# Two heads per quadrant and token pairs for q and k of the last two batches of an attention and highway kernel

## The chip, the cores and the metric

The kernel runs on one core of a Trainium2 chip. The metric is the device time of one execution in microseconds. Before the change it was 151.05 us, the median of 3 runs (151.03 to 151.7).

## The reference

Sliding-window attention with a linear distance bias, and then a highway layer on its output. Batch 8, 8 heads, 576 tokens, head dimension 64, all inputs and the output in float32.

```python
def _attn_ref(q, k, v):                       # each (8, 8, 576, 64)
    window = 128
    scale = 1.0 / np.sqrt(D)
    scores = scale * np.matmul(q, k.transpose(0, 1, 3, 2))
    rel = pos[:, None] - pos[None, :]
    slopes = 2.0 ** (-8.0 * (np.arange(H) + 1) / H)
    bias = slopes[:, None, None] * (-np.abs(rel))[None, :, :]
    mask = (rel >= 0) & (rel < window)
    scores = np.where(mask, scores + bias[None], -1e9)
    ...                                       # softmax over the last axis
    return np.matmul(attn, v)

def _moe_ref(x, w_h, w_t, b_t):               # x: (8 * 576, 512)
    H = np.maximum(x @ w_h, 0.0)
    T = 1.0 / (1.0 + np.exp(-(x @ w_t + b_t)))
    return T * H + (1.0 - T) * x
```

## The kernel before

**Staging.** The work on the attention side comes in units (b, s, g): batch b of 8, head group s of 2 (four heads each), token group g of 2. The highway side works on blocks (b, i) of 128 tokens, i = 0 to 3, and, for each pair of batches, a block i = 4 made of the first 64 tokens of both.

**Loading q and k.** For each (b, s, w), with w = 0 for q and 1 for k, one DMA on the queue of POOL (GpSimd) brings four heads into a tile `LD` of 128 partitions, converted to bf16 on the way. Partition 32a + p holds head 4s + a (a is the quadrant, 32 partitions) and the 18 tokens 18p to 18p + 17, so that each partition reads 4608 contiguous bytes. The text writes (b,s,q) and (b,s,k) for these loads. The values come in other DMAs on the same queue (`va`, L136), the weights in two (L140).

**Transposing.** `tr` (L184, written T(b,s,q) and T(b,s,k)) is one VectorE (DVE) instruction for each load. It transposes 32x32 blocks of 32-bit words (a word is two neighbouring bf16 of a token) inside each quadrant, 576 words per partition. Its output order is `"p (s t) -> p t s"` with t = 18: the 32 words of a block are written 18 words apart, so that the tokens end up in their natural order in `TR`.

**Attention on a unit.** `scores` (L227) multiplies on TensorE (PE) from `TR`, with 32 rows at a time; `soft` (L244) is the exponential on ScalarE (ACT) into `p`; `mask` (L249) multiplies `p` by the table `MT[s]` on DVE; `pv` (L260, L268, L281) is the product with the values on PE; `norm` on DVE takes the reciprocal of the sums (L294) and multiplies (L295) into the tile `X`, which empties a PSUM bank.

**Highway on a block.** `x_tr` (L321) transposes x on PE, `x_copy` (L326) copies it on ACT, `mm_h` (L331) and `mm_z` (L355, L357) or `mm_y` (L372) multiply by the weights on PE, `tanh` (L377) and `to_gate` (L381, or L385 on DVE) make the gate, `relu_sub` (L344, L347) and `gate` (L390) run on DVE, `add_x` (L394) on POOL (two of them on DVE, L399), and `store` issues the output DMA from SP.

**Order.** All of it is in one order written out by hand, the string `ORDER`: each letter takes the next item of its own list (L a load, T a transposition, s, e, m, p, n the steps of a unit, x, c, h, u, z, a, t, g, o, d those of a block), and a digit after it is the PSUM bank. Each engine works through its part of that order without overtaking, and waits come from the data that an instruction reads or overwrites, as written earlier in the order. POOL issues the loads and does the adds in this one order. The order of the loads is the list `LOADS`. Around the change these stand in this order (other letters left out, the numbers are places in `ORDER`):

```
L(5,1,k) 290, L(6,0,k) 294, T(5,0,k) 302, L(v) 306, T(5,1,q) 312, L(v) 314, L(6,1,q) 319, L(7,0,q) 321,
L(7,0,k) 326, T(5,1,k) 327, T(6,0,q) 330, T(6,0,k) 361, T(6,1,q) 378, L(v) 386, L(6,1,k) 392, L(7,1,q) 393,
L(7,1,k) 413, L(v) 419, L(v) 425, T(6,1,k) 428, L(v) 436, T(7,0,q) 449, T(7,0,k) 453, L(v) 456, T(7,1,q) 487, T(7,1,k) 495
```

L(6,0,q) stands earlier. The next instructions on DVE behind T(6,0,q) are those of `norm` of unit (4,1,0), which empties the bank that `x_tr` of block (3,3) writes.

**Buffers.** 20 `LD` tiles, 12 `TR`, 8 `p`, 5 `X`, and PSUM used as 8 banks.

Of the kernel before, what the change touches and what calls it, by code (L numbers as in the profile page):

```python
# [9 lines left out]
P = 128  # L10
NB, NS, NG = 8, 2, 2
NLD, NTR, NPB = 20, 12, 8

# [59 lines left out]
def kernel(  # L73
# [37 lines left out]

    LD = [cp.tile([P, NT * D], BF16, name=f"ld{i}") for i in range(NLD)]
    TR = [cp.tile([P, S, 2], BF16, name=f"tr{i}") for i in range(NTR)]
# [13 lines left out]
    def load(kind, *at):  # L127
        if kind == "t":
            b, s, w = at
            nc.gpsimd.dma_start(  # L130
                out=LD[(4 * b + 2 * s + w) % NLD][:],
                in_=(q, k)[w][b, 4 * s : 4 * s + 4].rearrange("h (p t) d -> (h p) (t d)", t=NT))
        elif kind == "v":
            b, n, m = at
            rows, h = min(P, S - m * P), b % 2 * H
            nc.gpsimd.dma_start(  # L136
                out=VA[b // 2][0:rows, h : h + n * H, m, 0:D],
                in_=v[b : b + n, :, m * P : m * P + rows].rearrange("b h p d -> p (b h) d"))
        elif at[0] < 2:
            nc.gpsimd.dma_start(  # L140
                out=(wH, wT)[at[0]][:],
                in_=(moe_w_h, moe_w_t)[at[0]].rearrange("(c p) n -> p c n", p=P))
        else:
            nc.gpsimd.dma_start(out=bT[0:1, :], in_=moe_b_t.rearrange("(o n) -> o n", o=1))

    def setup(part):
# [31 lines left out]
        else:  # L178
            s = part - 2
            nc.scalar.activation(out=MT[s][:], in_=PS[:, 4:8, 0:448], func=ACTF.Exp, scale=scale)  # L180

    def tr(b, s, w):
        i = 4 * b + 2 * s + w
        nc.vector.transpose(  # L184
            out=TR[i % NTR][:].rearrange("p s e -> p (s e)").bitcast(U32).rearrange(
                "p (s t) -> p t s", t=NT),
            in_=LD[i % NLD][:].bitcast(U32).rearrange("p (t i) -> p t i", i=32))

# [16 lines left out]

    def distances(s, g, bank):
        w = width(g)
        for a in range(4):
            nc.tensor.matmul(out=PS[:, bank + a, 0:w], lhsT=SI[:, 4 * s + a, :],
                             rhs=RB[:, 448 - w : 448], start=True, stop=False,  # L210
                             skip_group_check=True)

    def scores(b, s, g, bank):
        SB[b, s, g] = bank
        QT, KT = (TR[(4 * b + 2 * s + w) % NTR] for w in range(2))
        steps, parts = tiles(g)
        fresh = (b, s, g) not in by["pe_mask"]
        if not fresh:
            distances(s, g, bank)

        for step in steps:
            for e in range(2):
                for i, r in step:
                    c0, c1, k0, q0 = parts[i, r]
                    for a in range(4):
                        row = 32 * a
                        nc.tensor.matmul(  # L227
                            out=PS[r * D : r * D + D, bank + a, c0:c1],
                            lhsT=KT[row : row + 32, k0 : k0 + D, e],
                            rhs=QT[row : row + 32, q0 : q0 + c1 - c0, e],  # L230
                            start=fresh and e == 0, stop=e == 1,
                            tile_position=(row, r * D), skip_group_check=True)
            fresh = False
# [13 lines left out]
    def mask(b, s, g):  # L247
        p, w = PB[PT[b, s, g]], width(g)
        nc.vector.tensor_tensor(out=p[:, :, 0:w], in0=p[:, :, 0:w],  # L249
                                in1=MT[s][:, :, 448 - w : 448] if g else MT[s][:], op=ALU.mult)  # L250

    def pv(b, s, g, bank):
# [3 lines left out]
        for o in range(2):  # L256
            i = 2 * g + o
            p, col = piece(3 * i + 1)
            for a in range(4):
                nc.tensor.matmul(  # L260
                    out=PS[:, bank + o, a * E : a * E + E], lhsT=p[:, a, col : col + P],
                    rhs=VA[b // 2][:, b % 2 * H + 4 * s + a, i, :],
                    start=a == 0, stop=False, skip_group_check=True)
        if g == 0 and b % 2:
            for a in range(4):
                for r in range(2):
# [3 lines left out]
                        lhsT=PB[PT[b - 1 + r, s, 0]][:, a, 0:D],  # L270
                        rhs=VA[b // 2][:, r * H + 4 * s + a, 0, :],
                        start=False, stop=True, tile_position=(0, r * D), skip_group_check=True)
        for o in range(2):
            i = 2 * g + o
            for a in range(4):
                for row, pos, slot in ((0, 3 * i + 3, i + 1), (D, 3 * i, i - 1)):
                    if slot < 0:
# [5 lines left out]
                        lhsT=p[row : row + D, a, col : col + D],  # L283
                        rhs=VA[b // 2][row : row + D, b % 2 * H + 4 * s + a, slot, :],
                        start=False, stop=True, tile_position=(row, orow), skip_group_check=True)

    def norm(b, s, g):
        n = 6 if g == 0 and b % 2 else 4
        if (b, g) not in X:
            X[b, g] = xp.tile([P, NS, 2, 6, D], BF16, name="x")  # L290
        bank = AV.pop((b, s, g))
# [3 lines left out]
        nc.vector.tensor_tensor(  # L295
            out=X[b, g][:, s, :, 0:n, :], in0=av[:, :, 0:n, 0:D],
            in1=rd[:, :, 0:n, :].to_broadcast([P, 2, n, D]), op=ALU.mult)
# [15 lines left out]
    def like(ap, i):  # L313
        if i == 4:
            return ap.rearrange("p (c n) -> p c n", c=4)
        return ap.rearrange("p (s n) -> p s n", s=2)

# [22 lines left out]
    def relu_sub(b, i):  # L340
        uu = UU[b, i] = ft.tile([P, DM], BF16, name="uu")
        rr, pa = RR.pop((b, i), None), PA.pop((b, i), None)
        if rr is not None:
            nc.vector.tensor_tensor(out=like(uu[:], i), in0=like(rr[:], i), in1=xview(b, i),  # L344
                                    op=ALU.subtract)
        else:
            nc.vector.scalar_tensor_tensor(  # L347
                out=like(uu[:], i), in0=like(pa, i), scalar=0.0, in1=xview(b, i),
                op0=ALU.max, op1=ALU.subtract)
# [42 lines left out]
    def add_x(b, i):  # L392
        ot = OT[b, i] = ft.tile([P, DM], F32, name="ot")
        nc.gpsimd.tensor_tensor(out=like(ot[:], i), in0=like(UU.pop((b, i))[:], i),  # L394
                                in1=xview(b, i), op=ALU.add)

    def add_x_v(b, i):
        ot = OT[b, i] = ft.tile([P, DM], F32, name="ot")
        nc.vector.tensor_tensor(out=like(ot[:], i), in0=like(UU.pop((b, i))[:], i),  # L399
                                in1=xview(b, i), op=ALU.add)  # L400

    def store(b, i):
# [9 lines left out]
    do = dict(M=lambda s: distances(s, 0, 4), L=load, T=tr, S=setup, s=scores, e=soft, m=mask, p=pv, n=norm, x=x_tr, c=x_copy,  # L412
              h=mm_h, u=relu_sub, z=mm_z, a=tanh, t=to_gate, k=to_gate_v, r=relu, g=gate, o=add_x, d=store,
# [42 lines left out]
```

## Time and profile before

| | before |
|---|---|
| time, median of 3 runs (lowest, highest) | 151.05 us (151.03, 151.7) |
| the profiled execution: its time, its span | 151.79 us, 150.1 us |
| busy share of the span: PE, DVE, ACT, POOL | 87%, 88%, 80%, 59% |
| L184 transpositions on DVE | 32, 39.4 us in all, 1249 ns each |
| q and k loads (L130) | 32 of 288 KB each, 0.57 us of POOL to issue one, median 7 to 8 us from issue to landing |
| DMA packets | 48233, 38480 of them under 512 B |
| chain of waits, by engine | PE 46%, DVE 27%, DMA 17% |

The profile is one execution. PE is TensorE's matmuls, DVE VectorE, ACT ScalarE, POOL GpSimd. Times in the trace are microseconds from the start of the span; a busy share in the slices is in tenths, each slice being a fortieth of the span (3.75 us); the row PEclk is the clock granted to TensorE in tenths of full speed. In a timeline row come the start, the length, the engine, the source line, the operation, the tiles, the count, and in brackets the idle time of the engine before it and what ended it.

### The profile page before, as it was taken

What the parts mean: (1) busy time and instruction counts of PE and PEld (TensorE: products, weight loads), DVE (VectorE), ACT (ScalarE), POOL (GpSimd) and SP (SyncE); (2) the same over time, 40 slices, a digit from 0 to 9 for tenths busy, and PEclk for the clock granted to TensorE, in tenths of its full rate; (3) what the DMA queues carried; (4) which work ended last, traced back from release to release, by engine and by line L of the source; (5) the groups of instructions that cost most, each with busy time, mean ns of one, the idle gap of its engine ahead of it and who ended that gap; (6) DMA issues with size and microseconds to landing.
All of it is one profiled execution on the core that took longest, in us unless ns stands there. A gap on an engine that the chain in (4) does not pass through costs nothing.

```text
span 150.1 us, 5788 instructions
## 1 busy us (share of the span) xinstructions
PE 130.9 (87%) x2525; PEld 80.3 (54%) x2525; DVE 132.2 (88%) x226; ACT 119.3 (80%) x167; POOL 87.9 (59%) x102
## 2 busy tenths in 40 slices
PE   0477589969999999979999899997999999999960
PEld 0136465444666665655755556674557566555520
DVE  4974998759899999999969999999999999977882
ACT  5298369913999899769999979979799898899860
POOL 6977662195075851994159870859655035685640
PEclk9999999995999999999999999999999999999999
DMA  2999999999999999899999998399999121253544
GB/s 47 186 165 199 182 208 198 179 217 167 131 135 167 198 208 220 156 150 204 256 226 185 130 211 279 51 195 214 185 215 144 65 74 63 51 173 140 195 142 155
DMA packets 48233, 25.01 MB, mean 167 GB/s; under 512 B 38480, under 2 KB 39504, under 8 KB 48208
## 3 DMA queue, kind: packets, MB, share of 16 engines
q0 software_dynamic: 42960, 15.21, 96.6%
q1 hardware_dynamic: 5248, 9.44, 18.3%
q8 instruction: 19, 0.31, 0.9%
q14 instruction: 6, 0.05, 0.1%
HBM read 30.41 MB, written 9.44 MB: 266 GB/s over the span
## 4 chain that ended last, share of the span: by engine, by line
PE 46%; DVE 27%; DMA 17%; issue 3%; POOL 2%; ACT 2%; DVEq 0%; POOLq 0%; ACTq 0%
PE ps L331 14%; PE ps L355 8%; DMA va<-in_v_dram 8%; DVE x L295 6%; DVE p L249 6%; PE ps L372 6%; DMA ld<-in_q_dram 5%; DVE tr L184 5%; PE ps L227 5%; DMA ld<-in_k_dram 4%; PE ps L281 4%; DVE uu L390 3%; PE ps L321 3%; PE ps L260 3%; DVE uu L347 3%
## 5 line engine op out<-in xcount | busy, mean ns | idle before, releaser
L394 POOL TENSOR_TENSOR ot<-uu,x 128x512 f32<-128x512 bf16 x34 | 42.8, 1265 | 49.0 <-DVE uu L390 30.6
L244 ACT ACTIVATE p<-ps 128x1792 bf16<-128x1792 f32 (+1 forms) x32 | 50.0, 1562 | 12.2 <-PE ps L227 12.2
L184 DVE STREAM_TRANSPOSE tr<-ld 128x576 uint32<-128x576 uint32 x32 | 39.4, 1249 | 4.7 <-DMA ld<-in_q_dram 3.9
L331 PE MATMUL ps<-wH,xt 128*128 128x512 bf16 x144 | 37.3, 391 | 0.0
L249 DVE TENSOR_TENSOR p<-p,mt 128x1792 bf16<-128x1792 bf16 (+1 forms) x29 | 29.5, 1021 | 1.4 <-ACT p L244 1.4
L136 POOL DMA_DIRECT2D va<-in_v_dram x25 | 25.2, 1014 | 1.4 <-DMA ld<-in_q_dram 0.9
L295 DVE TENSOR_TENSOR x<-ps,rd 128x512 bf16<-128x512 f32 (+1 forms) x32 | 24.3, 758 | 1.3
L355 PE MATMUL ps<-wT,xt 128*128 128x512 bf16 x96 | 25.2, 386 | 0.0
L326 ACT COPY xt<-ps 128x512 bf16<-128x512 bf16 x36 | 21.0, 586 | 3.5 <-PE ps L321 3.3
L377 ACT ACTIVATE tt<-ps 128x512 f16<-128x512 f32 x36 | 21.5, 604 | 2.9 <-PE ps L372 1.6
L227 PE MATMUL ps<-tr,tr 32*64 32x192 bf16 (+2 forms) x1280 | 20.2, 248 | 1.3 <-DVE tr L184 1.3
L331 PEld LDWEIGHTS <-xt 128*128 128x128 bf16 x144 | 13.3, 100 | 14.3 <-issue 1.7
L227 PEld LDWEIGHTS <-tr 32*64 32x64 bf16 x1280 | 16.6, 112 | 6.6 <-DVE tr L184 2.9
L260 PE MATMUL ps<-va,p 128*128 128x65 bf16 x256 | 13.9, 198 | 4.7 <-DMA va<-in_v_dram 2.1
L260 PEld LDWEIGHTS <-p 128*128 128x128 bf16 x256 | 11.7, 100 | 9.4 <-DVE p L249 2.7
L347 DVE SCALAR_TENSOR_TENSOR uu<-ps,x 128x512 bf16<-128x512 f32 x22 | 14.9, 685 | 2.0 <-PE ps L331 1.8
L390 DVE TENSOR_TENSOR uu<-uu,tt 128x512 bf16<-128x512 bf16 x36 | 15.9, 454 | 0.2
L381 ACT ACTIVATE tt<-tt 128x512 f16<-128x512 f16 x25 | 15.7, 634 | 0.1
L321 PE MATMUL ps<-ident,x 128*128 128x128 bf16 x144 | 13.9, 224 | 2.0 <-DVE x L295 1.8
L321 PEld LDWEIGHTS <-x 128*128 128x128 bf16 x144 | 10.2, 99 | 8.7 <-issue 2.7
L281 PE MATMUL ps<-va,p 64*64 64x65 bf16 x448 | 14.7, 200 | 0.0
L355 PEld LDWEIGHTS <-xt 128*128 128x128 bf16 x96 | 8.2, 99 | 8.1 <-issue 0.8
(46 smaller groups left out, 116.8 us busy)
## 6 DMA issues: line engine op xcount, KB each, us to landing
out_dram<-ot SPq DMA_DIRECT2D x32, 256.0 KB, 4.1
ld<-in_q_dram POOLq DMA_DIRECT2D x16, 288.0 KB, 7.9
ld<-in_k_dram POOLq DMA_DIRECT2D x16, 288.0 KB, 7.2
va<-in_v_dram POOLq DMA_DIRECT2D x12, 256.0 KB, 7.7
va<-in_v_dram POOLq DMA_DIRECT2D x11, 128.0 KB, 7.9
out_dram<-ot SPq DMA_DIRECT2D x8, 128.0 KB, 2.8
wT<-in_moe_w_t_dram POOLq DMA_DIRECT2D x1, 512.0 KB, 8.9
wH<-in_moe_w_h_dram POOLq DMA_DIRECT2D x1, 512.0 KB, 10.8
```

Source lines behind the costliest of these rows:

```text
L136: nc.gpsimd.dma_start(out=VA[b // 2][0:rows, h : h + n * H, m, 0:D], in_=v[b : b + n, :, m * P : m * P + rows].rearrange("b h p d -> p (b ...
L184: nc.vector.transpose(out=TR[i % NTR][:].rearrange("p s e -> p (s e)").bitcast(U32).rearrange("p (s t) -> p t s", t=NT), in_=LD[i % NLD][: ...
L227: nc.tensor.matmul(out=PS[r * D : r * D + D, bank + a, c0:c1], lhsT=KT[row : row + 32, k0 : k0 + D, e], rhs=QT[row : row + 32, q0 : q0 + c ...
L244: nc.scalar.activation(out=PB[i][:, :, 0:w], in_=PS[:, bank : bank + 4, 0:w], func=ACTF.Exp, scale=scale)
L249: nc.vector.tensor_tensor(out=p[:, :, 0:w], in0=p[:, :, 0:w], in1=MT[s][:, :, 448 - w : 448] if g else MT[s][:], op=ALU.mult)
L260: nc.tensor.matmul(out=PS[:, bank + o, a * E : a * E + E], lhsT=p[:, a, col : col + P], rhs=VA[b // 2][:, b % 2 * H + 4 * s + a, i, :], st ...
L295: nc.vector.tensor_tensor(out=X[b, g][:, s, :, 0:n, :], in0=av[:, :, 0:n, 0:D], in1=rd[:, :, 0:n, :].to_broadcast([P, 2, n, D]), op=ALU.mult)
L321: nc.tensor.transpose(out=XP[b, i][:, c * P : (c + 1) * P], in_=xchunk(b, i, c), identity=ident[:])
L331: nc.tensor.matmul(out=pa, lhsT=XT[b, i][:, c, :], rhs=wH[:, c, :], start=c == 0, stop=c == NC - 1)
L355: nc.tensor.matmul(out=pz, lhsT=xt[:, c, :], rhs=wT[:, c, :], start=c == 0, stop=False)
L377: nc.scalar.activation(out=tt[:], in_=PZ.pop((b, i)), func=ACTF.Tanh, scale=0.5)
L394: nc.gpsimd.tensor_tensor(out=like(ot[:], i), in0=like(UU.pop((b, i))[:], i), in1=xview(b, i), op=ALU.add)
```

## The change

For batches 6 and 7 (`NBW` = 6) the layout of q and k on the chip changes; for the others nothing does.

- A load (b, s, w) is now two DMAs, one for each of the quadrants a = 2s and 2s + 1. Quadrant a holds the two heads 2a and 2a + 1, one in each half s of the tile. Partition 32a + p holds the token pairs 64t + 2p, 64t + 2p + 1 for t = 0 to 8, so that a contiguous run is two tokens: 512 bytes read, 256 written. `LD` becomes 10 tiles of double width (both s of one tensor).
- The transposition (b, s, w) reads half s of all four quadrants, which the loads (b, 0, w) and (b, 1, w) bring together. It writes the words of a block 2 words apart.
- Head a of group s is now 2a + s instead of 4s + a: `head()` picks the slopes, the mask table's rows (`MT` becomes one tile for all 8 heads, read with a step of two heads) and the values; `X` of these batches puts the two heads side by side, and its views have fewer and longer runs.
- `ORDER` and `LOADS` are kept as they are.

```diff
-NLD, NTR, NPB = 20, 12, 8
+NLD, NTR, NPB, NBW = 20, 12, 8, 6
...
-    LD = [cp.tile([P, NT * D], BF16, name=f"ld{i}") for i in range(NLD)]
+    LD = [cp.tile([P, NS, NT * D], BF16, name=f"ld{i}") for i in range(NLD // 2)]
...
-    MT = [cp.tile([P, 4, 448], BF16, name=f"mt{s}") for s in range(NS)]
+    MT = cp.tile([P, H, 448], BF16, name="mt")
...
             b, s, w = at
-            nc.gpsimd.dma_start(
-                out=LD[(4 * b + 2 * s + w) % NLD][:],
-                in_=(q, k)[w][b, 4 * s : 4 * s + 4].rearrange("h (p t) d -> (h p) (t d)", t=NT))
+            ld, src = LD[(2 * b + w) % (NLD // 2)], (q, k)[w][b]
+            if b < NBW:
+                nc.gpsimd.dma_start(
+                    out=ld[:, s, :],
+                    in_=src[4 * s : 4 * s + 4].rearrange("h (p t) d -> (h p) (t d)", t=NT))
+                return
+            for a in (2 * s, 2 * s + 1):
+                nc.gpsimd.dma_start(
+                    out=ld[32 * a : 32 * a + 32, :, :].rearrange("p s (t x) -> p (s t) x", x=2 * D),
+                    in_=src[2 * a : 2 * a + 2].rearrange("h (t p j) d -> p (h t) (j d)", p=32, j=2))
...
     def tr(b, s, w):
         i = 4 * b + 2 * s + w
-        nc.vector.transpose(
-            out=TR[i % NTR][:].rearrange("p s e -> p (s e)").bitcast(U32).rearrange(
-                "p (s t) -> p t s", t=NT),
-            in_=LD[i % NLD][:].bitcast(U32).rearrange("p (t i) -> p t i", i=32))
+        to = TR[i % NTR][:].rearrange("p s e -> p (s e)").bitcast(U32)
+        ld = LD[(2 * b + w) % (NLD // 2)][:, s, :].bitcast(U32)
+        if b < NBW:
+            nc.vector.transpose(out=to.rearrange("p (s t) -> p t s", t=NT),
+                                in_=ld.rearrange("p (t i) -> p t i", i=32))
+        else:
+            nc.vector.transpose(out=to.rearrange("p (t s j) -> p t j s", s=32, j=2),
+                                in_=ld.rearrange("p (t j i) -> p t j i", j=2, i=32))
+
+    def head(b, s, a):
+        return 4 * s + a if b < NBW else 2 * a + s
...
     def mask(b, s, g):
...
-                                in1=MT[s][:, :, 448 - w : 448] if g else MT[s][:], op=ALU.mult)
+                                in1=(MT[:, 4 * s : 4 * s + 4] if b < NBW else MT[:, s::2])[
+                                    :, :, 448 - w : 448], op=ALU.mult)
...
     def norm(b, s, g):
...
-            X[b, g] = xp.tile([P, NS, 2, 6, D], BF16, name="x")
+            X[b, g] = xp.tile([P, NS, 2, 6, D] if b < NBW else [P, 2, 6, NS, D], BF16, name="x")
...
-            out=X[b, g][:, s, :, 0:n, :], in0=av[:, :, 0:n, 0:D],
+            out=X[b, g][:, s, :, 0:n, :] if b < NBW else X[b, g][:, :, 0:n, s, :], in0=av[:, :, 0:n, 0:D],
...
     def xchunk(b, i, c):
+        if b >= NBW:
+            x = X[b, 0][:, c // 2, 4 + c % 2] if i == 4 else X[b, i // 2][:, i % 2, c]
+            return x.rearrange("p s d -> p (s d)")
...
     def xview(b, i):
+        if b >= NBW and i == 4:
+            return X[b, 0][:, :, 4:6, :, :].rearrange("p o t s d -> p o (t s d)")
+        if b >= NBW:
+            return X[b, i // 2][:, i % 2, 0:4, :, :].rearrange("p t s d -> p (t s d)")
```

More of the change, by code (lines that the diff above doesn't have):

```diff
@@ L204, in tiles, with distances @@
         return [[(i, r) for r in range(2)] for i in (2 * g, 2 * g + 1)] + [[last]], parts
-    def distances(s, g, bank):
+    def distances(b, s, g, bank):
         w = width(g)
         for a in range(4):
-            nc.tensor.matmul(out=PS[:, bank + a, 0:w], lhsT=SI[:, 4 * s + a, :],
+            nc.tensor.matmul(out=PS[:, bank + a, 0:w], lhsT=SI[:, head(b, s, a), :],
                              rhs=RB[:, 448 - w : 448], start=True, stop=False,
@@ L218, in scores @@
         if not fresh:
-            distances(s, g, bank)
+            distances(b, s, g, bank)
         for step in steps:
@@ L283, in pv @@
                         lhsT=p[row : row + D, a, col : col + D],
-                        rhs=VA[b // 2][row : row + D, b % 2 * H + 4 * s + a, slot, :],
+                        rhs=VA[b // 2][row : row + D, b % 2 * H + head(b, s, a), slot, :],
                         start=False, stop=True, tile_position=(row, orow), skip_group_check=True)
@@ L311, in xview, with like @@
         return X[b, i // 2][:, :, i % 2, 0:4, :].rearrange("p s t d -> p s (t d)")
[L313 to L316, printed above, removed]
+    def like(ap, b, i):
+        if b >= NBW and i < 4:
+            return ap
+        n = 4 if b < NBW and i == 4 else 2
+        return ap.rearrange("p (s n) -> p s n", s=n)
     def x_tr(b, i, bank):
@@ L343, in relu_sub @@
         if rr is not None:
-            nc.vector.tensor_tensor(out=like(uu[:], i), in0=like(rr[:], i), in1=xview(b, i),
+            nc.vector.tensor_tensor(out=like(uu[:], b, i), in0=like(rr[:], b, i), in1=xview(b, i),
                                     op=ALU.subtract)
@@ L347, in relu_sub @@
             nc.vector.scalar_tensor_tensor(
-                out=like(uu[:], i), in0=like(pa, i), scalar=0.0, in1=xview(b, i),
+                out=like(uu[:], b, i), in0=like(pa, b, i), scalar=0.0, in1=xview(b, i),
                 op0=ALU.max, op1=ALU.subtract)
@@ L410, in store @@
             nc.sync.dma_start(out=out[row : row + D, :], in_=ot[r * D : (r + 1) * D, :])
-    do = dict(M=lambda s: distances(s, 0, 4), L=load, T=tr, S=setup, s=scores, e=soft, m=mask, p=pv, n=norm, x=x_tr, c=x_copy,
+    do = dict(M=lambda s: distances(0, s, 0, 4), L=load, T=tr, S=setup, s=scores, e=soft, m=mask, p=pv, n=norm, x=x_tr, c=x_copy,
               h=mm_h, u=relu_sub, z=mm_z, a=tanh, t=to_gate, k=to_gate_v, r=relu, g=gate, o=add_x, d=store,
```

10 lines of the change are left out of this document (5 added, 5 removed).

## The prediction

> **What bounds the kernel now.** I read the page's slices first, then busy time by stretch, then the timelines of DVE, PE and POOL around the first transposition that the change touches, and last the loads that feed it. The slices:
>
> ```profile
> PE   0477589969999999979999899997999999999960
> DVE  4974998759899999999969999999999999977882
> PEclk9999999995999999999999999999999999999999
> DMA  2999999999999999899999998399999121253544
> ```
>
> PE and DVE are both full from about 38 us to 140 us; the loads (DMA) end near 116 us. Busy time by stretch (PE, PEld, DVE, ACT, POOL, granted clock):
>
> ```profile
> 84.18:104.35 20.17, 18.55 (x361) 11.32 (x360) 19.91 (x36) 17.81 (x25) 12.83 (x13) 1.00 1.21 185
> 104.35:144.10 39.75, 39.75 (x669) 23.96 (x669) 36.63 (x68) 34.59 (x53) 21.10 (x18) 1.00 0.67 128
> ```
>
> From 104.35 us PE has no idle time until 144.1 us, and the chain of waits runs through PE there. So nothing that DVE saves after 104 us moves the end, and every delay of PE at 104 us moves it one for one. From 84.18 to 104.35 us DVE is full (19.91 of 20.17) and PE idles 1.62 us; nearly all of that is three waits for DVE:
>
> ```profile
> 83.79 1.90 PE L331 MATMUL ps<-wH,xt 128*128 128x512 bf16 x8
> 86.22 0.38 PE L321 MATMUL ps<-ident,x 128*128 128x128 bf16 x4 [0.54 <-DVE x L295]
> ...
> 87.75 0.38 PE L321 MATMUL ps<-ident,x 128*128 128x128 bf16 x4 [0.28 <-DVE uu L347]
> ...
> 104.35 0.38 PE L321 MATMUL ps<-ident,x 128*128 128x128 bf16 x4 [0.79 <-DVE x L295]
> ```
>
> **Step 1, the new wait.** A load of batches 6 and 7 now brings two quadrants (64 partitions) of both head groups, so a transposition of all 128 partitions needs both loads of its tensor, s=0 and s=1. The order is kept, and in it the first transposition of batch 6, T(6,0,q), stands directly behind T(5,1,k); together they are the L184 x2 at 83.09, the second one starting at 84.18. The load that it now needs as well, (6,1,q), is issued late:
>
> ```profile
> 83.09 2.33 DVE L184 STREAM_TRANSPOSE tr<-ld 128x576 uint32<-128x576 uint32 x2
> 85.26 0.17 DVE L294 RECIPROCAL rd<-ps 128x8 f32<-128x8 f32 x1
> 85.48 0.69 DVE L295 TENSOR_TENSOR x<-ps,rd 128x512 bf16<-128x512 f32 x1
> ```
>
> ```profile
> 79.82 2.03 POOL L136 DMA_DIRECT2D va<-in_v_dram  x2
> 81.84 1.11 POOL L130 DMA_DIRECT2D ld<-in_q_dram  x2
> ```
>
> The DMA view of 81.9 to 82.3 us, which holds this issue alone, gives its time to landing in the last column:
>
> ```profile
> ld<-in_q_dram POOLq DMA_DIRECT2D x1, 288.0 KB, 6.5
> ```
>
> 81.84 + 6.5 = 88.3 us. It is now two DMAs, each with 32 partitions x 18 runs = 576 packets of 512 B read and 256 B written, instead of one of 128 packets of 4608 B. The nearest rows are 2.5 us of value loads alone (256 B read, 128 B written) and 2 us of q and k loads alone:
>
> ```profile
> DMA packets 2995, 0.40 MB, mean 159 GB/s; under 512 B 2994, under 2 KB 2994, under 8 KB 2994
> ...
> DMA packets 198, 0.43 MB, mean 217 GB/s; under 512 B 16, under 2 KB 16, under 8 KB 197
> ```
>
> So 1,200 small packets or 90 large ones pass per us. A pair of 1,152 packets takes 0.96 us if a packet costs what the small one does, 1.92 us if twice that; the large load took 128 / 90 = 1.42 us. The difference lies between -0.46 and +0.5 us; by bytes it is nil, which I take, with +0.1 for the second issue: landing at 88.4 us. (The Trainium skill, "SBUF — State Buffer", Door 1, speaks against the new shape: 32 partitions reach 8 of the 16 DMA ports, 189 GB/s at 1 MiB. By that the pair's 288 KB would take an estimated 1.56 us and the sum would grow by 0.1 us; no row here has such a shape.)
>
> T(6,0,q) thus starts at 88.4 instead of 84.18 us: 4.2 us in which DVE stands. Behind it in DVE's order are L294 and L295, which empty a PSUM bank; PE's transposes at 86.22 write that bank, and after 85.69 us PE has nothing else in order. ACT and POOL run dry behind both.
>
> **Step 2, the transposition itself.** Today 576 words take 1.25 us, written 18 words apart, near two cycles a word. DVE rows at one element a cycle (L295: 512 elements 692 ns, 768 elements 958 ns) give 1.04 ns an element, so 0.60 us plus a fixed part of 0.05 to 0.16. Bounds 0.65 and 1.25 us (I see nothing in a step of 2 words that could make it slower than 18); I take 0.70, the rows at one per cycle, hence 0.55 us saved each, eight times. The next DVE instruction started 1.08 us after T(6,0,q) did; now 0.53. So it starts at 88.93 instead of 85.26: **+3.7 us**. Of the other seven savings only T(6,0,k) and T(6,1,q) (89.46, 93.24 us) lie before 104 us, 1.1 us of lead for DVE; the five later ones, 2.75 us, lie beside a full PE and are worth nothing.
>
> T(6,0,k) is not held up: its second load, (6,1,k), stands behind it in the order kept, so it takes two of its four quadrants from what lies in the buffer (batch 1's k), and the load then follows it. T(6,1,k), T(7,0,q), T(7,0,k) start at 104.21, 107.80 and 108.89; the later loads of their pairs land at 101.6 to 106.6, each 2.3 us or more earlier, and step 5 takes at most 1.5 us of that.
>
> **Step 3, PE's clock.** PE now idles from 85.69 to 86.22 + 3.7 = 89.9 us, 4.2 us. The trace has a smaller pause with its consequence (three stretches of 3.4 us):
>
> ```profile
> 30.19:33.60 3.41, 1.93 (x65) 1.66 (x72) 1.66 (x3) 0.55 (x2) 3.41 (x4) 1.00 1.11 219
> 33.60:37.01 3.41, 3.41 (x47) 1.53 (x40) 3.38 (x6) 1.45 (x1) 2.29 (x3) 0.50 1.96 168
> ...
> 63.40:66.80 3.40, 2.37 (x76) 1.85 (x75) 3.34 (x6) 1.99 (x3) 3.40 (x5) 1.00 0.99 148
> ```
>
> With PE busy 1.93 of 3.41 us the next 3.41 us ran at clock 0.50; with 2.37 of 3.40 it did not. A pause of 4.2 us leaves some such stretch busy for less than 1.93 us wherever its limits fall. In the slow stretch eight L331 and the scores ahead took 3.28 and 0.78 us where they take 1.90 and 0.55 elsewhere: 1.6 us lost. I take **+1.6**; with the slow stretch partly inside the pause it is 0.8, with 5 us of slow work 2.4. (The Trainium skill, "TensorE: Matmul & The Clock Gate", Part 1, gives 3.4 us windows that run freely against the kernel's start; the rows of this trace fit that, and it leaves the phase open.)
>
> **Step 4, what comes back.** Of the three PE waits the second and third (0.28 + 0.79) end when DVE has more lead than PE. DVE gains 1.1 us and PE's clock costs PE more than DVE, so both vanish: **-1.1**.
>
> **Step 5, the rest.** POOL issues eight more DMAs. 128 packets cost it 0.57 us (L130) and 512 packets 0.75 (L140, the weights), so two of 576 cost 1.5 instead of 0.57, +0.95 per load. For (6,0,k) it falls into POOL's idle 1.51 us before 78.00; for (6,0,q) at 61.0 into 4.93 us of idle before 74.29; for (7,0,q) and (7,0,k) it delays two adds by 2.8 us while DVE stands; for the last three the 2.58 us before 99.42 take most. What is left meets the v load whose landing is tightest: issued at 102.24, 9.6 us to landing, 111.85; the first P·V matmul of batch 6 starts at 112.71. Lead 0.86 us against 0.5 to 1.5 us: 0 to 0.7 us, I take 0.1. Nothing for the mask's strided operand (L249 on rows of 384 out of 448 costs 949 against 1080 ns, the share of its elements), for the new x layout (L295's runs of 64 elements stay contiguous, source PSUM as before), or for the X views, which only get fewer runs.
>
> **Sum.** +3.7 + 1.6 - 1.1 + 0.1 = +4.3 us. The profiled execution took 151.79 us (span 150.1, 1.7 around it), 0.5% above the median of 151.05; on its own time the sum is 156.1, on the median 155.3. A measurement here can tell about 0.5%, 0.76 us.
>
> **Rivals.**
> 1. The wait grows (chance 0.15): packets cost twice the small one (+0.5 at T(6,0,q), and up to +0.5 at T(5,0,q), which already waits 1.35 us for a load at 76.35), the v load adds 0.7, slow clock 2.4. +3.7 + 1.0 + 2.4 - 1.1 + 0.7: 157.8. For it: the load queue is full there. Against: by bytes the load is unchanged.
> 2. The wait without the clock's price (0.13): +3.7 - 1.1: 153.7. It needs a landing some 1.5 us earlier or a lucky phase; packets at 84 to 86 us ran at 760 per us instead of 1,200, which could fall elsewhere.
> 3. The transposition doesn't get shorter (0.10): +4.2 + 1.6 - 0.8: 156.0.
> 4. Other side, faster (0.04): the pair lands before DVE asks. Then DVE's 1.65 us of three savings fills PE's 1.6 us of idle: 149.4. It breaks even if DVE stands 1.6 us at most (1.1 of shift), a landing by 85.8 us, 4.0 us after the issue; the fastest q or k load in the trace took 4.1 and this one stands behind two v loads.
> 5. A stay within 0.5% (0.03): landing near 86.5, clock untouched.
>
> The forecast itself has 0.55. The range 152.9 to 157.6 takes in the forecast with its bounds, rivals 2 and 3 and half of rival 1; it leaves out about 0.15. Faster 0.04, same 0.03, slower 0.93.
>
> **What would show it.** L184 x8 near 0.70 us; one DVE idle of about 4.2 us before the 25th transposition, ended by ld<-in_q_dram; PE idle as long, then a stretch at clock 0.50; PE without a gap afterwards. Wrong if the 25th transposition starts by 85.8 us, if L184 stays at 1.25 us, or if a second wait of over 1 us stands behind 104 us.

## The result and the profile after

The changed kernel takes 161.26 us (median of 4 runs, 159.6 to 162.89), the kernel before 151.38 us (median of 4 runs on the same chip, 151.03 to 151.71). The ratio is 1.0617 [1.0524, 1.071]: slower by 9.3 us, where +4.3 us was forecast. (Executions fall into two states, and the ratios here and below compare those in the faster one; the medians take all.) The profiled execution took 160.94 us, with a span of 158.9 us against 150.1. The lines below follow the steps of the prediction. First the slices of the page of the changed kernel:

```profile
PE   0467599999996999999993049999899999999970
DVE  4965997799979999997980089599998898977882
PEclk9999999999999999999999556999999999999996
DMA  3999999999999998999999983099999310253344
```

Nothing is different in kind from the forecast: one hole in PE and DVE (slices 22 to 24 of 3.97 us each, 83 to 95 us), and a clock at half speed across its end. But the hole is twice as wide as forecast. The DVE timeline across it:

```profile
81.68 1.25 DVE L194 STREAM_TRANSPOSE tr<-ld 128x576 uint32<-128x576 uint32 x1
91.90 0.78 DVE L197 STREAM_TRANSPOSE tr<-ld 128x576 uint32<-128x576 uint32 x1 [8.96 <-DMA ld<-in_k_dram]
92.60 0.17 DVE L309 RECIPROCAL rd<-ps 128x8 f32<-128x8 f32 x1
```

The 25th transposition, T(6,0,q), starts at 91.90 us instead of 84.18. The bracket names the k load, but what lands last ahead of 91.90 is the pair (6,1,q), seen in the timeline of POOL and in the DMA view of 80.9 to 81.3 us:

```profile
80.42 2.62 POOL L137 DMA_DIRECT2D ld<-in_q_dram  x4
```

```profile
ld<-in_q_dram POOLq DMA_DIRECT2D x2, 144.0 KB, 10.6
```

The four issues are the pairs (6,1,q) and (7,0,q). The first pair is issued at 80.42 and 81.08 us, earlier than the single load before (81.84), and lands 10.6 us later, at 91.0 and 91.7; before it was 6.5 us. PE, from its timeline:

```profile
83.03 1.90 PE L354 MATMUL ps<-wH,xt 128*128 128x512 bf16 x8
93.55 0.59 PE L344 MATMUL ps<-ident,x 128*128 128x128 bf16 x4 [8.62 <-DVE x L310]
93.93 1.91 PE L354 MATMUL ps<-wH,xt 128*128 128x512 bf16 x4
...
98.68 0.39 PE L344 MATMUL ps<-ident,x 128*128 128x128 bf16 x4
...
113.21 0.38 PE L344 MATMUL ps<-ident,x 128*128 128x128 bf16 x4 [0.79 <-DVE x L310]
```

Four mm_h matmuls take 1.91 us behind the pause, where the kernel before shows 1.03 for four (and 1.90 for eight):

```profile
86.44 1.03 PE L331 MATMUL ps<-wH,xt 128*128 128x512 bf16 x4
...
89.70 0.39 PE L321 MATMUL ps<-ident,x 128*128 128x128 bf16 x4
```

The stretches (length; busy us of PE, PEld, DVE, ACT, POOL; the granted clock; the DMA share and GB/s):

```profile
84.20:87.61 3.41, 0.72 (x4) 0.21 (x3) 0.00 (x0) 1.18 (x2) 2.77 (x3) 1.00 4.09 94
87.61:91.03 3.42, 0.00 (x0) 0.00 (x0) 0.00 (x0) 0.00 (x0) 0.00 (x0) 0.50 2.62 140
91.03:94.44 3.41, 0.89 (x6) 0.61 (x6) 2.51 (x6) 0.27 (x1) 0.48 (x1) 0.50 1.14 212
94.44:97.85 3.41, 3.41 (x13) 1.48 (x12) 3.41 (x6) 1.93 (x4) 2.42 (x2) 0.50 0.28 84
97.85:101.27 3.42, 3.42 (x79) 2.22 (x78) 2.82 (x7) 2.65 (x4) 0.15 (x1) 1.00 0.20 77
113.21:153.00 39.79, 39.79 (x670) 24.01 (x670) 35.48 (x68) 34.62 (x54) 21.98 (x18) 1.00 0.69 129
```

Three stretches in turn are under-used (0.72, 0.00 and 0.89 us busy) and each is followed by one at clock 0.50; the first full one, 94.44 to 97.85, is followed by 1.00. (The Trainium skill, "TensorE: Matmul & The Clock Gate", Part 1, says that the gate goes to half after an idle window of some 3.4 us and back to full after a busy one, the windows running freely. The trace agrees on the length: the changes at 87.61 and 97.85 lie three times 3.41 us apart. A window need not be wholly idle, though: those with 0.72 and 0.89 us of work led to half clock too.) From 113.21 us to 153 PE is full, as it was before from 104.35. The two kinds of transposition, from the page's groups:

```profile
L194 DVE STREAM_TRANSPOSE tr<-ld 128x576 uint32<-128x576 uint32 x24 | 29.8, 1248 | 5.5 <-DMA ld<-in_q_dram 5.1
...
L197 DVE STREAM_TRANSPOSE tr<-ld 128x576 uint32<-128x576 uint32 x8 | 6.0, 765 | 9.0 <-DMA ld<-in_k_dram 9.0
```

So the spans, 150.1 and 158.9 us, differ as follows (the steps of PE from its timelines):

| term | forecast | measured | from |
|---|---|---|---|
| T(6,0,q) starts later | +4.2 | +7.72 | 84.18, 91.90 |
| it and the gap behind it are shorter | -0.55 | -0.38 | next DVE instruction 1.08 us later before, 0.70 now |
| slow clock | +1.6 | +1.93 | 93.55 to 98.68 is 5.13; before 86.22 to 89.70 is 3.48, of it 0.28 a wait |
| PE's two later waits | -1.1 | -0.28 | 0.28 has gone, 0.79 is still there at 113.21 |
| rest | +0.1 | -0.2 | the difference to +8.8 |

### The profile page after: what moved, and what is told of

Its sections match the earlier page's. It is cut to its first block, busy times and chain, and to the rows that moved or that the text cites. A ratio compares the mean times of both kernels' runs of the same rounds, so it can differ in the third digit from the quotient of the medians.

```text
span 158.9 us, 5802 instructions
## 1 busy us (share of the span) xinstructions
PE 132.1 (83%) x2525; PEld 81.2 (51%) x2525; DVE 129.5 (81%) x226; ACT 119.7 (75%) x167; POOL 94.7 (60%) x110
## 4 chain that ended last, share of the span: by engine, by line
PE 38%; DVE 23%; DMA 23%; POOL 11%; issue 2%; ACT 1%; DVEq 0%; POOLq 0%; ACTq 0%
DMA ld<-in_q_dram 17%; PE ps L354 11%; PE ps L378 7%; DVE tr L194 6%; DMA ld<-in_k_dram 6%; POOL va L143 5%; DVE x L310 5%; PE ps L395 5%; DVE p L263 4%; PE ps L241 4%; PE ps L344 4%; PE ps L296 3%; PE ps L275 3%; POOL ld L137 2%; POOL ot L417 2%
## 5 line engine op out<-in xcount | busy, mean ns | idle before, releaser
L417 POOL TENSOR_TENSOR ot<-uu,x 128x512 f32<-128x512 bf16 x34 | 43.4, 1281 | 50.9 <-DVE uu L413 31.5
L194 DVE STREAM_TRANSPOSE tr<-ld 128x576 uint32<-128x576 uint32 x24 | 29.8, 1248 | 5.5 <-DMA ld<-in_q_dram 5.1
L344 PE MATMUL ps<-ident,x 128*128 128x128 bf16 x144 | 14.4, 229 | 9.8 <-DVE x L310 9.8
L354 PEld LDWEIGHTS <-xt 128*128 128x128 bf16 x144 | 13.5, 101 | 13.7 <-issue 1.1
L413 DVE TENSOR_TENSOR uu<-uu,tt 128x512 bf16<-128x512 bf16 x36 | 14.9, 428 | 0.2
L197 DVE STREAM_TRANSPOSE tr<-ld 128x576 uint32<-128x576 uint32 x8 | 6.0, 765 | 9.0 <-DMA ld<-in_k_dram 9.0
```

What stands on the lines that cost most here:

```text
L194: nc.vector.transpose(out=to.rearrange("p (s t) -> p t s", t=NT), in_=ld.rearrange("p (t i) -> p t i", i=32))
L344: nc.tensor.transpose(out=XP[b, i][:, c * P : (c + 1) * P], in_=xchunk(b, i, c), identity=ident[:])
L354: nc.tensor.matmul(out=pa, lhsT=XT[b, i][:, c, :], rhs=wH[:, c, :], start=c == 0, stop=c == NC - 1)
L417: nc.gpsimd.tensor_tensor(out=like(ot[:], b, i), in0=like(UU.pop((b, i))[:], b, i), in1=xview(b, i), op=ALU.add)
```

## The experiments

The first theory is the prediction's: the wait for (6,1,q) and the clock behind the pause are the whole loss, and what they cost depends on when the load lands. Against it stands that the new shape of the loads (32 partitions, 512-byte runs) costs time of its own, and that the new transposition isn't shorter or not worth anything. In every kernel the place to look at is the same: the start of the 25th transposition, the idle time ahead of it, and PE behind it.

### The wait by itself, the wait taken away, the transposition by itself

**wait_alone**: the kernel before, with (6,0,q) and (6,1,q) exchanged in the list of loads, so that T(6,0,q) waits for a load that is issued where (6,1,q) is.

```diff
-LOADS = (..., 40, 47, 38, ..., 42, 41, 52, 56, ...)
+LOADS = (..., 40, 52, 38, ..., 42, 41, 47, 56, ...)
```

> The kernel before with two loads exchanged in the order of loads: (6,1,q) takes the early place and (6,0,q) the late one that was issued at 81.84 us. Layout, packets and transpositions as before; only T(6,0,q) now needs a load issued at about 81.8 us. Theory A (the wait itself, DVE then PE's clock): landing near 88.3 us, DVE idle some 4 us ahead of the 25th transposition, PE idle as long, a stretch at clock 0.50, 155 to 157 us. Theory B (the split loads are what makes the wait of the changed kernel long: DVE idle 8.96 us there, load 10.6 us under way): the same 4 us here, so about half of the changed kernel's loss. If instead this run idles near 9 us and takes 159 us or more, the packets are innocent and B falls.

158.39 us against 151.76, ratio 1.0428 [1.0365, 1.049], above the 155 to 157 us expected. The DVE timeline, the DMA view of 81.4 to 81.7 us and the PE timeline:

```profile
88.50 1.26 DVE L184 STREAM_TRANSPOSE tr<-ld 128x576 uint32<-128x576 uint32 x1 [4.60 <-DMA ld<-in_q_dram]
```

```profile
ld<-in_q_dram POOLq DMA_DIRECT2D x1, 288.0 KB, 7.1
```

```profile
90.56 0.58 PE L321 MATMUL ps<-ident,x 128*128 128x128 bf16 x4 [5.30 <-DVE x L295]
...
95.90 0.39 PE L321 MATMUL ps<-ident,x 128*128 128x128 bf16 x4
```

The load lands at 88.5 us, which is the prediction's 88.4. PE starts again at 90.56 after 5.30 us of idle; the clock is at half from 88.5 to 95.3 us, and the same stretch of PE's work (90.56 to 95.90) takes 5.34 us instead of 3.20: 2.1 us. The later wait, that at 104 us in the kernel before, is 0.79 us here too. So with the old large packets the forecast's landing is right, and the wait with its clock costs 6.5 us of the 9.3. About 2.9 us (1.9% between the two ratios) belong to the rest of the change.

**pair_early**: the changed kernel with (6,1,q) loaded directly behind (5,1,q).

```diff
-LOADS = (..., 43, 44, 45, 46, 48, 42, 41, 52, 56, ...)
+LOADS = (..., 43, 44, 45, 52, 46, 48, 42, 41, 56, ...)
-ORDER: "...p6aLds0anoh5t..."  "...yLts0naLaLgz4u..."
+ORDER: "...p6aLLds0anoh5t..."  "...yLts0naaLgz4u..."
```

> The changed kernel with one load moved: the two DMAs of (6,1,q) are issued directly behind (5,1,q), near 68 us instead of 81. Everything else of the change stays, the 8 split loads and the short transpositions included. Theory A: the wait at T(6,0,q) is gone (landing near 80 us), PE's clock stays at 1.00 until the end, and 150.5 to 152.5 us. Theory B (split loads slow the queue wherever they stand): DVE or PE waits for loads elsewhere between 75 and 115 us, 154 us or more.

152.62 us against 151.76, ratio 1.009 [1.0033, 1.0147], just above the 152.5 us of Theory A. The transposition starts at 84.55 us with no wait, and the clock stays at full. PE's timeline shows what is left, two waits longer than before near 90 us (0.56 and 0.91 us, where before had one of 0.28) and, further on, the old one of 0.79 us:

```profile
88.20 0.38 PE L344 MATMUL ps<-ident,x 128*128 128x128 bf16 x4 [0.56 <-DVE uu L370]
...
91.56 0.30 PE L275 MATMUL ps<-va,p 128*128 128x65 bf16 x4 [0.91 <-DMA va<-in_v_dram]
```

Nearly the whole loss goes with the one load's place in the queue. What is left is a value load that now stands behind the pair and lands at 91.51 us.

**step2_alone** and **step2_all**: the kernel before with only the new output order of the transposition, in batches 6 and 7 or in all. Their tokens come out in another order, so these two show a time and not a usable kernel.

```diff
-            out=....rearrange("p (s t) -> p t s", t=NT),
-            in_=....rearrange("p (t i) -> p t i", i=32))
+            out=....rearrange("p (t s j) -> p t j s", s=32, j=2),   # b >= 6, or all b
+            in_=....rearrange("p (t j i) -> p t j i", j=2, i=32))
```

> The kernel before with only the transposition's output step changed in batches 6 and 7 (2 words instead of 18); loads and layout as before, so their tokens come out in another order, which leaves the times of everything else alone. Theory A (PE is the bound behind 104 us): L184 765 ns in 8 of 32, 3.9 us of DVE saved, of it 0 to 1.1 us at the end: 150.0 to 151.5 us. Rival (DVE is the bound there): 147 to 149 us.

> As the run with the output step alone, but in all 32 transpositions (token order changed in all batches). 32 x 0.48 = 15.5 us of DVE saved. Theory A (PE nearly full from 60 us on): 1 to 4 us off, 147 to 150 us. Rival (DVE the bound from 38 us on): 8 us or more off, under 143 us.

151.78 and 150.59 us against 151.76, ratios 0.996 [0.9909, 1.0012] and 0.9954 [0.9908, 1.0001]: half a per cent less, which neither interval parts from no change, and for step2_all less than the 1 to 4 us of Theory A. The groups of step2_all, then the DVE and the PE timeline of it (its lines behind the transposition have numbers four higher than before):

```profile
L184 DVE STREAM_TRANSPOSE tr<-ld 128x576 uint32<-128x576 uint32 x32 | 24.3, 768 | 8.5 <-DMA ld<-in_q_dram 6.6
```

```profile
96.08 0.23 DVE L298 RECIPROCAL rd<-ps 128x12 f32<-128x12 f32 x1 [0.28 <-ACT xt L330]
```

```profile
102.69 0.38 PE L325 MATMUL ps<-ident,x 128*128 128x128 bf16 x4 [0.78 <-DVE x L299]
```

768 against 1249 ns, 32 times: 15.4 us less work on DVE, and by the ratio the time moves by 0.7 us. PE is the bound, as the stretches of before said. The second of these lines explains a term of the forecast: DVE idled just ahead of 96.08 us, waiting for ACT (and through it for PE), and from there its order is full up to the norm that PE waits for. A lead that DVE gains earlier is lost at that point, so the wait stays at 0.78 us. What makes the wait is one relu_sub behind that point: in the kernel before it takes 1.38 us (first line below); in quads_long, described further down, the same step takes 0.42 (second line), and there PE doesn't wait:

```profile
102.08 1.38 DVE L344 TENSOR_TENSOR uu<-rr,x 128x512 bf16<-128x512 bf16 x1
```

```profile
110.33 0.42 DVE L367 TENSOR_TENSOR uu<-rr,x 128x512 bf16<-128x512 bf16 x1
```

Why this one instruction takes so long in all the other kernels isn't shown.

### The shape of the loads, and the clock by itself

**changed_again** is the changed kernel once more, as the measure for the other three. **wait_small_runs** is wait_alone with the eight loads of batches 6 and 7 in 512-byte runs on all 128 partitions; **wait_halves** is wait_alone with each of them as two DMAs of 64 partitions with the long runs:

```diff
+                out=ld[:].rearrange("p (n y) -> p n y", n=9)[:, :, 0:128],     # wait_small_runs
+                in_=src.rearrange("h (p n j) d -> (h p) n (j d)", n=9, j=2))
...
+            for i in range(1 if b < 6 else 2):                                 # wait_halves
+                n = 4 if b < 6 else 2
+                nc.gpsimd.dma_start(
+                    out=ld[32 * n * i : 32 * n * (i + 1), :],
+                    in_=src[n * i : n * i + n].rearrange("h (p t) d -> (h p) (t d)", t=NT))
```

**kept_warm** is the changed kernel with 110 matmuls of 112 columns, whose result nobody reads, ahead of the transposes that wait:

```diff
+            if step == "h" and at["h"] == 15:
+                for _ in range(110):
+                    nc.tensor.matmul(out=PS[:, 6, 400:512], lhsT=SI[:, 0, :], rhs=RB[:, 0:112], ...)
```

> The changed kernel once more, beside the three that follow. All theories: 160 to 162 us, DVE idle about 9 us ahead of the 25th transposition, PE's clock at 0.50 for some 10 us.

> The run with the wait alone, and the 8 loads of batches 6 and 7 each as one DMA of 128 partitions with runs of 512 B (1152 packets instead of 128; the tile is padded so that the runs stay apart; transpositions still write 18 words apart). Theory B1 (the small packets make the second half of the wait): the late load lands 2 to 3 us later than with the wait alone, DVE idle 7 to 8 us, 160 to 161 us. Theory B2 (it is the 32 or 64 partitions of a DMA, or the number of DMAs): as the wait alone, 157.5 to 159 us, DVE idle 4 to 5 us.

> The run with the wait alone, and the 8 loads of batches 6 and 7 each as two DMAs of 64 partitions with the large packets of before. Theory B1 (small packets): as the wait alone, 157.5 to 159 us, DVE idle 4 to 5 us. Theory B2 (half the partitions, twice the DMAs): DVE idle 7 to 8 us, 160 to 161 us.

> The changed kernel with 110 idle matmuls of 112 columns (their result is not used) ahead of the place where PE stands for DVE. The load's wait is as in the changed kernel. Theory A (the clock is a cost of its own): no stretch at 0.50 until the end, 1.5 to 2.5 us faster than the changed kernel, 158 to 159.5 us. Rival (DVE's stand hides PE's slow stretch): same time as the changed kernel within 0.5 us, clock at 1.00 all the same.

The kernel before took 151.06 us beside these.

| | time, us | ratio | (6,1,q)'s place lands | T(6,0,q) starts | half clock |
|---|---|---|---|---|---|
| changed_again | 160.43 | 1.0643 [1.0561, 1.0725] | 89.7, 90.2 | 90.36 | 90.6 to 97.4 |
| wait_small_runs | 158.41 | 1.0497 [1.0445, 1.055] | 89.4 | 89.45 | 89.6 to 96.5 |
| wait_halves | 157.92 | 1.0486 [1.042, 1.0551] | 88.4, 88.8 | 88.87 | 88.1 to 94.9 |
| kept_warm | 157.62 | 1.0458 [1.0398, 1.0517] | 89.4, 90.0 | 90.21 | none |

The changed kernel's own landing moves from profile to profile: 91.7 us the first time, 90.2 now. Short runs alone put the landing 0.9 us behind wait_alone's 88.5, two halves 0.3 us; neither reaches the changed kernel, so neither of the theories B1 and B2 holds by itself. kept_warm's timeline of PE:

```profile
85.19 5.57 PE L451 MATMUL ps<-rb,si 128*128 128x112 bf16 x110
91.86 0.38 PE L344 MATMUL ps<-ident,x 128*128 128x128 bf16 x4 [0.24 <-DVE x L310]
92.08 1.03 PE L354 MATMUL ps<-wH,xt 128*128 128x512 bf16 x4
93.39 0.38 PE L344 MATMUL ps<-ident,x 128*128 128x128 bf16 x4 [0.28 <-DVE uu L370]
```

The same wait (the transposition starts at 90.21 us after 5.36 us of idle), but PE's next matmuls take 1.03 us and not 1.91. From the transposition to the end of the span it is 65.4 us, in changed_again 67.5: the clock by itself costs 2.1 us in the profiles, and 2.8 us between the medians.

### Few partitions, and the queue ahead

**quads_long** is the changed kernel without the token pairs (32 partitions as before, but runs of 4608 bytes, and the old transposition). **wait_halves_small** is wait_halves with 512-byte runs. The two tell apart whether small packets and few partitions together make the late landing (B3 in the expectations) or few partitions are enough (B4).

```diff
-                    out=ld[32 * a : 32 * a + 32, :, :].rearrange("p s (t x) -> p (s t) x", x=2 * D),
-                    in_=src[2 * a : 2 * a + 2].rearrange("h (t p j) d -> p (h t) (j d)", p=32, j=2))
+                    out=ld[32 * a : 32 * a + 32, :, :],                        # quads_long
+                    in_=src[2 * a : 2 * a + 2].rearrange("h (p t) d -> p h (t d)", t=NT))
...
+                    out=ld[64 * i : 64 * i + 64].rearrange("p (n y) -> p n y", n=9)[:, :, 0:128],
+                    in_=src[2 * i : 2 * i + 2].rearrange("h (p n j) d -> (h p) n (j d)", n=9, j=2))  # wait_halves_small
```

**ahead_of_values** is the changed kernel with (6,1,q) moved ahead of the two value loads only; **both_early** is pair_early with (6,1,k) early as well, so that T(6,0,k) finds all four quadrants. In the changed kernel, and in every variant with its loads but both_early, T(6,0,k) runs ahead of (6,1,k) and takes two quadrants of batch 1's k, as the prediction says; those kernels leave out that wait and part of batch 6's result.

```diff
-LOADS = (..., 46, 48, 42, 41, 52, 56, ...)
+LOADS = (..., 46, 48, 52, 42, 41, 56, ...)            # ahead_of_values
-LOADS = (..., 45, 52, 46, 48, 42, 41, 56, 57, 50, 53, ...)
+LOADS = (..., 45, 52, 46, 48, 53, 42, 41, 56, 57, 50, ...)   # both_early, with its L in ORDER
```

> The changed kernel without the token pairs: the loads of batches 6 and 7 still come as two DMAs of 32 partitions with two heads each (so T(6,0,q) still needs both loads), but with runs of 4608 B (64 packets each), and the transposition writes 18 words apart again. Theory B3 (small packets together with few partitions make the late landing): last landing near 88.5 to 89 us as with the halves, DVE idle 4.5 to 6.5 us, 157.5 to 158.5 us. Theory B4 (a DMA of 32 partitions is enough): last landing 90 us or later, 160 us or more.

> The run with the wait alone, and the 8 loads of batches 6 and 7 each as two DMAs of 64 partitions with runs of 512 B, 576 packets each: number, size and bytes of packets as in the changed kernel, but each partition's runs lie next to each other in memory and not 16 KB apart. Theory B3 (small packets with half the partitions): last landing 90 us or later, 159.5 to 161 us. Theory B5 (the 16 KB between the runs): landing near 89.4 as in the run with small packets, 158 to 159 us.

> The changed kernel with the two DMAs of (6,1,q) issued ahead of the two value loads that stand in front of them (79.8 us on), nothing else moved. Theory A with the queue as the cause of the late landing (1024 + 2048 packets stand in front): landing at 84.5 to 86 us, DVE idle 1 to 3 us, 153 to 155.5 us. Rival (a split load takes 9 to 10 us by itself): landing 88 us or later, 157 us or more.

> The kernel with the pair (6,1,q) issued early, and (6,1,k) issued directly behind (6,0,k) as well, so that T(6,0,k) finds all four quadrants filled. Theory A: that costs little, 152 to 153.5 us, as long as the load lands before 89.9 us. Rival (the queue there is full): DVE waits at T(6,0,k), 154 us or more.

The kernel before took 151.66 us beside these.

| | time, us | ratio | (6,1,q)'s place lands | T(6,0,q) starts | half clock |
|---|---|---|---|---|---|
| quads_long | 159.73 | 1.059 [1.0497, 1.0683] | 89.5, 90.1 | 90.33 | 87.6 to 97.8 |
| wait_halves_small | 159.01 | 1.0456 [1.031, 1.0603] | 88.2, 89.0 | 89.10 | 90.2 to 97.1 |
| ahead_of_values | 155.06 | 1.0289 [1.0191, 1.0387] | 85.1, 86.3 | 86.53 | 89.5 to 92.9 |
| both_early | 154.6 | 1.0266 [1.017, 1.0361] | ahead of the start | 85.20 | none there |

quads_long has 128 packets for the pair, like the load of before, and lands as late as changed_again: a late landing doesn't need short runs, as B4 had it (its 160 us or more was missed by 0.3 us). Halves with short runs stay at 89.0 us, though the times of that kernel scatter from 156.8 to 161.5 us and carry little weight. The DMA views of quads_long (81.6 to 82.5 us) and of wait_halves (80 to 81 us):

```profile
ld<-in_q_dram POOLq DMA_DIRECT2D x2, 144.0 KB, 8.0
```

```profile
ld<-in_q_dram POOLq DMA_DIRECT2D x2, 144.0 KB, 8.4
```

The issue to landing is no longer in the one than in the other; quads_long merely issues 1.6 us later (81.51 against 79.94). So the two times don't show by themselves what the shape costs. wait_alone is the closer partner: its two value loads and the load itself are issued at 79.39, 80.25 and 81.42 us, quads_long's value loads and first DMA at 79.49, 80.36 and 81.51, and still the one lands at 88.5 us and the others at 89.5 and 90.1. The completion marks of the 16 DMA engines, which the trace keeps for each DMA, say more. A DMA has landed with the last of 16:

| pair (6,1,q) or its place | issued | 8th engine | last engine |
|---|---|---|---|
| wait_alone, 128 partitions, long runs | 81.42 | 87.4 | 88.5 |
| wait_halves, second DMA | 80.47 | 87.8 | 88.8 |
| quads_long, second DMA | 82.04 | 87.9 | 90.1 |
| changed_again, second DMA | 81.90 | 88.8 | 90.2 |
| changed kernel, second DMA | 81.08 | 89.8 | 91.7 |

Half of the engines are done with quads_long's pair at 87.9 us, hardly later than in wait_halves; the last is 2.3 us behind. Over all loads issued from 77 to 83 us the last engine lies on average 1.1 to 1.5 us behind the 8th in the kernels with 64 or 128 partitions, and 1.8 to 3.4 in those with 32 (kept_warm is an exception with 1.0). The value loads ahead of the pair show it too: the one directly ahead of it has 87.4 for the 8th engine and 90.4 for the last in the changed kernel, 86.7 and 87.2 in the one before. With short runs the 8th engine is later as well (88.8 and 89.8). In the changed kernel's two profiles that is the larger part: against wait_alone the 8th engine is 1.4 and 2.4 us later and the lag behind it 0.2 and 0.8 us longer, while in quads_long it is 0.5 and 1.2.

The trace keeps the time of each packet too. The short packets of the q and k loads took 102 ns each on average from 87 to 90 us in the changed kernel, 64 in changed_again and 59 to 110 in the other kernels with the changed loads; packets of the same size took 41 in wait_small_runs and wait_halves_small, on 128 and 64 partitions. The long packets of quads_long took 221 ns from 85 to 88 us, those of wait_alone 217. So in these profiles the slow packets come with short runs and 32 partitions together, and in quads_long the longer lag comes with 32 partitions alone.

Whether the shape is the cause isn't settled: between 60 and 72 us the lag is 1.5 to 3.0 us in every kernel but wait_halves_small (0.9), the one before too (2.9), and behind 95 us it is 1.1 in the changed kernel, which has 32-partition loads there as well (2.3 in quads_long). kept_warm has the changed loads and a lag of only 0.7 us at its pair, which lands at 90.0 us with issues 1.1 us later than in changed_again. What is shown is that most kernels with 32 partitions still have a lagging engine when the pair lands, and the others mostly don't. The trace doesn't say which engine it is.

ahead_of_values saves 5.4 us of the changed kernel's loss (155.06 against 160.43, each beside its own runs of the kernel before) by passing two value loads: DVE still stands 2.86 us and PE 2.98, with one slow stretch behind it. both_early costs more than pair_early, for another reason; Theory A's 152 to 153.5 us is missed, though DVE doesn't wait at T(6,0,k) as the rival had it. Its timelines of POOL and DVE:

```profile
85.68 0.66 POOL L137 DMA_DIRECT2D ld<-in_k_dram  x1 [0.65 <-issue]
87.03 0.66 POOL L137 DMA_DIRECT2D ld<-in_k_dram  x1 [0.69 <-DVE x L310]
87.71 3.37 POOL L417 TENSOR_TENSOR ot<-uu,x 128x512 f32<-128x512 bf16 x3
```

```profile
88.91 0.69 DVE L370 SCALAR_TENSOR_TENSOR uu<-ps,x 128x512 bf16<-128x512 f32 x1 [1.21 <-POOL ot L417]
```

The adds that start at 84.38 us in pair_early start at 87.71: two more issues stand ahead of them on POOL (1.3 us), and POOL idles 2.2 us between its issues instead of 0.2. relu_sub on DVE waits 1.21 us for the add, and PE waits 1.59 us for relu_sub. Of the 1.5 us between the two spans (153.0 and 151.5) 0.65 lies ahead of T(6,0,q), which starts at 85.20 instead of 84.55; what makes this part was not found (both_early's profile has a stretch at clock 0.50 from 33.8 to 37.2 us, as that of before has, and pair_early's has none). (The intervals of the two don't overlap, though they ran beside different runs of the kernel before.) That is step 5 of the prediction in another place: POOL's issue time is free only while nobody waits for an add.

## Why the prediction was wrong in size

The direction, the mechanism and the places were right: the new wait of T(6,0,q), the pause of PE, the half clock, a full PE behind it. pair_early and kept_warm take away one part each and the time follows. 161.26 us lies above the range (157.6) because one term was mis-sized and two smaller ones added to it.

- **Step 1, the landing: the term that failed.** It was put at 88.4 us: the old load's 6.5 us under way, plus a packet price between -0.46 and +0.5 us from rates at other places. The old load at that place does land at 88.5 (wait_alone). The new pair lands at 90.2 and 91.7 in two profiles, though its issues are done about as early, and T(6,0,q) started 7.7 us later instead of 4.2. The sum put two things at nothing. The packets of the pair and of the loads beside it took 64 to 102 ns from 87 to 90 us, where the same packets on more partitions took 41, which goes with an 8th engine 1.4 to 2.4 us later than wait_alone's; and the last engine came 1.3 to 1.9 us behind the 8th instead of 1.1. The prediction had seen slow packets at 84 to 86 us, but counted them only as something that might fall elsewhere (rival 2). Why they stay slow for longer here is open. The prediction also weighed a rule of the Trainium skill ("SBUF — State Buffer", Door 1: 32 partitions reach 8 of 16 ports), estimated at +0.1 us. The same section gives 32 and 64 partitions nearly the same rate; the 8th engines of quads_long and wait_halves (87.9 and 87.8 us) fit that and the landings (90.1 and 88.8) don't, but quads_long's pair was also issued later, so no run here settles what the rule is worth.
- **Step 2, the transposition.** 765 ns against 700 forecast, inside the bounds; the next instruction follows after 0.70 us instead of 0.53. That it is worth nothing behind 104 us is shown by step2_all.
- **Step 3, the clock.** 1.9 us in the changed kernel, 2.5 in changed_again (92.01 to 97.68 against 3.20 us), 2.1 in wait_alone, against 1.6 with bounds of 0.8 and 2.4. The 1.6 was read off a slow stretch of one length; here PE resumed inside a slow stretch and went through a second whole one, 4.3 us of slow work.
- **Step 4, what comes back.** Of 1.1 us only 0.28 did, and that by the slow clock: kept_warm, at full clock, still waits 0.28 us at 93.39. The 0.79 us is there in every kernel but quads_long (which waits 0.92 us at 121.09 instead), since a relu_sub of 1.38 us instead of 0.42 makes it, behind a point where DVE is itself released by the x copy (in every variant; the kernel before has no idle time there). That the wait was named "for DVE" did not make it one that DVE's earlier lead could fill.
- **Step 5, the rest.** POOL took 0.66 us for an issue of 576 packets (0.75 forecast), the v load's margin held, and there is no wait behind 104 us but the old one. Right, for this order; both_early shows the same cost on the path in another.
- **Rivals.** Rival 1 (the wait grows, 157.8) was the nearest, and its dearer packets did come; but its +0.5 us for them was too little and its late value load didn't come, so it is still 3.5 us short. Rivals 2 to 5 fell: the clock had its price, the transposition is shorter, and the pair didn't land before DVE asked. Rival 4 counted a gain even beside its own condition: pair_early meets that, with no wait left, and is 0.9% slower and not faster, so DVE's savings filled no idle of PE there.

No kernel of these beats the one before. The only one with the new loads in which every transposition has all its data, both_early, is 2.7% slower.

## What to carry to other kernels

When a change makes an instruction wait for a transfer that was needed later until now, move the transfer first: its place in the queue was worth some 8 of the 9 us here (pair_early), the faster instruction nothing. Then count again what each moved load delays: with both loads early 4 us were left. Don't price a new transfer shape by bytes or by a packet rate from another place; look at how slow packets are where it will stand, and give the landing at least the spread that the trace's completions show. An engine's saved time counts only up to the next point where that engine itself waits for the bound one.

## What was not expected of the hardware

- One pause of 8.6 us left the granted clock at 0.50 for 10.2 us (87.61 to 97.85), one of 2.98 us in ahead_of_values for 3.4 us. PE's slow work was only the part after it resumed, up to two stretches.
- Within one of these DMAs the 16 engines finish 1 to 3 us apart, and the value loads queued ahead of a pair lag in the same way.
- In the changed kernel value packets of 256 bytes read took 107 to 146 ns, averaged over each microsecond from 83 to 89 us, where elsewhere they mostly take 32. Every kernel has slower passages of that kind near 41, 62 and 84 us. The last one (packets at more than 1.5 times their usual time) is 2 to 4 us long in the kernel before and in the runs with more partitions or long runs, and 4 to 7 us in those with the changed loads. What causes them was not found.
